# Linear attention, RMS norm and a GELU feed-forward in block products: operand addresses, and GpSimd's work moved between the two layers

## The chip, the core and the metric

The kernel runs on one core of a Trainium2 chip. What counts is the device time of one execution in microseconds, on this one core. Four engines work side by side and meet through semaphores: TensorE (PE; matmuls, with the weight loads that precede them), VectorE (DVE), ScalarE (ACT) and GpSimd (POOL). SyncE (SP) issues most of the DMA transfers. Every engine takes its instructions in program order.

## The reference

```python
# attention: 8 batches, 8 heads, 576 tokens, 64 features a head
kv = np.einsum('bhsd,bhse->bhde', k, v)
out = np.einsum('bhsd,bhde->bhse', q, kv)
rms = np.sqrt(np.mean(out * out, axis=-1, keepdims=True) + 1e-06)
attn = out / rms * g_norm
# feed-forward on the 8*576 = 4608 tokens, 512 features, 2048 hidden
x = attn.transpose(0, 2, 1, 3).reshape(4608, 512)
h = x @ w_in
g = 0.5 * h * (1.0 + erf(h / sqrt(2)))
result = g @ w_out
```

All of it is in 32-bit floats. Nearly all arithmetic is in the two products with `w_in` (512x2048) and `w_out` (2048x512).

## The kernel before

**Precision.** Each float32 factor is split into a high part and the low rest (`hi`, `lo`; a cast on ScalarE, a subtraction on VectorE or GpSimd). A product is then three matmuls: hi x hi, lo x hi, hi x lo.

**Chunks.** The 4608 tokens are nine chunks `c` of 512. Chunks 0 and 1 (`PLAIN` = 2) use plain matmuls of 512 columns for both layers (L655 and L682). From chunk 3 (`FAST` = 3) on, both layers use a Strassen-Winograd scheme: a product of 2x2 blocks in seven block products. Its operands are sums and differences of blocks, and the results are added up again. Chunk 2 is between: its first layer is in block products (`layer1_pair`), its second is plain, and beside it the operands for the later chunks' second layer are made from `w_out`: `sum_out` on GpSimd, `split_out` (a cast on ScalarE, L1199, and a low on VectorE, L1200), and `send`, which writes them to device memory from ScalarE's DMA queue.

**A chunk from 3 on.** Its *first layer* has eight pairs `j`. Each has a `first_part` (block products 0 to 3) and a `second_part` (4 to 6), staggered: first part of `j`, then second part of `j-1`. All their matmuls are at L523, in `product`: 128 weights columns, 256 moving columns. VectorE adds up the results (`add`, L514; the first result is copied out of PSUM at L560) and ScalarE applies the GELU (L579). The *second layer* (class `Fast`) has 28 *ticks* of 12 matmuls each (L1140); a tick is one block product `k` for a quarter `n` of the hidden features, in the order `TICKS`. Ahead of a tick, `ready` makes its operand: `hi` on ScalarE (L1117), `lo` on VectorE (L1118). `combine` (L1107) makes the sums among the hidden blocks.

**The next chunk** is prepared meanwhile. Within the first layer (`within_layer1`, called after each second part): its projections (attention's `q` times `kv`, L230; the split of `q` has its low on GpSimd, L217), their squares (ScalarE, L240, L241; summed on VectorE, L253), the inverse root (`rsqrt`, small VectorE operations at L277 to L295), and the scaling (`scale`: VectorE spreads the factors by a transpose, L307, GpSimd multiplies, L303). Within the second layer (`within_layer2`): the sums of its blocks (`add_blocks`, L344, four operations on GpSimd at tick 0), and seven pieces (`next_piece`: cast on ScalarE, L349, low at L354, on VectorE for an even piece and on GpSimd for an odd one).

**Weights.** Products of weights come back from device memory through a ring of six tiles (`RING`): when a tile is used up, `fetch` loads the next but five into it, on SyncE's queue. Ring tiles have 48 elements more than others. An operand of the first layer lies 48 elements into its tile, one of the second layer 16. Some products stay in memory (`RESIDENT`), in whatever tiles `take` finds free.

The order is written by hand: each engine's instructions follow the program text. Tiles get their addresses in the order in which they are first used.

Of the kernel before, what the change touches and what calls it, by code (L numbers as in the profile page):

```python
# [37 lines left out]
def linear_attn_rms_gelu_ffn(  # L38
# [63 lines left out]
    def late_tile(name):  # L102

        if name not in late:
            late[name] = const.tile([P, 2 * DM], I32, name=name).bitcast(F32)
        return late[name]
# [19 lines left out]
    def load_kv(b, p):  # L126
# [10 lines left out]
        if b == 0:  # L137
            tails = late_tile(f"w_in{NF - 1}")[:TAIL].rearrange("p (a n) -> p a n", a=NP)
            if p == 0:
                nc.sync.dma_start(out=tails, in_=kv_tail[0])  # L140
            tail = tails[:, p]
        else:
            if early:
                tail = late_tile(f"w_in{NF - 5}")[:, (p - 2) * 2 * P:(p - 1) * 2 * P]
            elif b == PLAIN + 1 and p > 1:
                if p == 2:
                    kv_ps["tails"] = const.tile([P, 2 * DM], F32, name="w_in12")
# [37 lines left out]
    class Attn:  # L185
# [7 lines left out]
        def load(self, k):  # L193
# [6 lines left out]
            elif self.c == 1 and k:  # L200
                q = const.tile([P, 2 * DM], I32, name=f"w_in{NF - 1}").bitcast(F32)
# [6 lines left out]
        def split_q(self, p, eng=nc.gpsimd):  # L208
            q = self.q.pop(p)
            if self.c > PLAIN and p % 2:  # L210
                t = const.tile([P, 2 * DM], F32R, name="w_in4")
# [101 lines left out]
        def high_x(self, p):  # L313
            x = const.tile([P, 2, CH], F32R, name=f"x{(NP * self.c + p) % 6}")
            nc.scalar.copy(out=x[:, 0], in_=self.o[p])  # L315
            self.x[p] = x
# [64 lines left out]
    def product_out(at, src, eng=nc.sync):  # L381

        key, n = at[:-1], at[-1]
        if key in RESIDENT and key[0] == "out":
            if key not in resident:
                resident[key] = take(F32R)[1]
# [37 lines left out]
    def high_sums():  # L424

        for (j, second), s in stage.items():
            if j % 2:
                t = reused(second, F32R).rearrange("p (k a n) -> p k a n", k=2, a=2)
            else:
                t = const.tile([P, 2, 2, HALF], F32R, name=f"x{2 + second}")  # L430
# [32 lines left out]
    RESIDENT += [("out", k, GROUPS - 1) for k in ORDER]  # L463
    resident = {}
# [13 lines left out]
    def fetch(n):  # L478

        if n < len(queue):  # L480
# [3 lines left out]
            away = AWAY if key[0] == "in" else AWAY // 3  # L484
# [15 lines left out]
    def take(dtype=F32):  # L500
        name = free.pop(0)
        return name, const.tile([P, 2 * DM], dtype, name=name)

    def keep(key):
        name, t = take(F32R)
        resident[key] = t
# [47 lines left out]
    def first_part(at, j):  # L554
# [5 lines left out]
        nc.vector.tensor_copy(out=u[:, left], in_=a[:, left])  # L560
# [336 lines left out]
    def spread_work(c, i):  # L897
# [31 lines left out]
        for n in {12: (0,), 13: (4, 5), 14: (1, 2), 15: (3, 6)}.get(i, ()):  # L929
            names[c + 1, n] = ("x2", "x3", *(f"w_in{m}" for m in range(5, 10)))[n]  # L930
            t = const.tile([P, 2 * DM], F32R, name=names[c + 1, n])
# [340 lines left out]
    def within_layer1(c, j):  # L1272
# [3 lines left out]
        aft = attn[c + 2] if c + 2 < NCH else None  # L1276
        if nxt:
            if j < NP:
                nxt.project(j, bank("a0"))
                nxt.squares(j)  # L1280
                if j < 2:
                    nxt.split_q(2 + j)
            if j == NP:
                ps = bank("a0")
                nxt.inv = nxt.rsqrt(nxt.fold(ps))
        if c + 2 < B:
            if j == 2:
                kv_ps[c + 2, 0] = bank("a1")
                sum_kv(c + 2, (0, 1), kv_ps[c + 2, 0])
            if j in (2, 3):  # L1290
                load_kv(c + 2, j)
            if j == 5:
                sum_kv(c + 2, (2, 3), kv_ps[c + 2, 0])
                split_kv(c + 2, range(NP))
        if aft:
# [4 lines left out]
        if nxt and j in (5, 6):  # L1300
            nxt.scale(2 * j - 9, nc.gpsimd)
        if c == FAST and j < 2:
            send()
            raw_out(NJ2 - 2 + j)
            free.extend(f"w_out{NF - 4 + 2 * j + n}" for n in range(2))
# [8 lines left out]
    def within_layer2(c, layer, i):  # L1314
# [5 lines left out]
        if c + 1 < NCH:  # L1320
            step = len(layer.ticks) // 8
            if i == 0:
                for k in ("T3", "T1", "T2", "T4"):
                    attn[c + 1].add_blocks(k, nc.gpsimd)
            if i % step == step - 1 and i // step < NPR:
                n = i // step
                next_piece(c, n, nc.gpsimd if n % 2 else nc.vector)

    free += ["x4", "x5", "x0", "x1", "w_in12"]
    for c in range(PLAIN, FAST):  # L1330
        for j in range(NJ2):
            s = c * NF + 2 * j
            pair = layer1_pair(attn[c], j, [lambda e=e: ahead(c, j, e) for e in range(2)])
# [16 lines left out]
            if c == FAST - 1:  # L1350
                if j:
                    free.extend(f"w_out{n}" for n in (2 * j - 2, 2 * j - 1) if n < NF - 4)
                if j == 1:
                    free.append(names.pop("g"))
                send()
                if j > 3:
                    keep(RESIDENT[j - 4])
            ahead_loads(c, j)
    for c in range(FAST, NCH):
# [3 lines left out]
        for j, second in parts_of_layer1():  # L1363
            if not second:
                first_part(at, j)
                if (c, j) == (FAST, 0):
# [4 lines left out]
                    free.extend(f"w_in{n}" for n in (13, 14, 15))  # L1371
# [68 lines left out]
```

## Time and profile before

| | |
|---|---|
| runs, median (lowest to highest) | 842.97 us (842.86 to 845.91), 3 runs |
| the profiled execution's own time | 843.54 us |
| its span, first to last instruction | 841.8 us |
| GpSimd busy in the span | 267.8 us (32%) |
| DMA queue of SyncE (q1) | 235.96 MB, 79.4% of 16 engines |
| TensorE's granted clock | 1.000 |

Up to about 316 us the span holds the splitting of the weights and chunks 0 to 2. Chunk 3 begins then; from there each chunk takes some 90 us, half of it per layer. A profile row names a group of instructions by line, engine, operation and tiles, with its count, busy time and mean duration. A timeline row gives the start, the duration of the group (matmuls overlap, so the distance of starts, not the duration of one, says how fast they follow each other), and in brackets how long the engine had been idle before, and what released it.

### The profile page before, as it was taken

Reading aid. Unit: us, or ns where it says so; the run is one execution under the profiler, and the core shown is the slowest. Engines: PE = TensorE matmul, PEld = TensorE weight load, DVE = VectorE, ACT = ScalarE, POOL = GpSimd, SP = SyncE. Lnnn points to the kernel's source line nnn. Section 1 sums busy time; section 2 is a strip of 40 time slices with the busy share of each in tenths; the row PEclk is TensorE's granted clock in tenths of the full one; section 3 lists DMA queues with packets and bytes.
Section 4 is the critical chain, followed back from the end, with each engine's and each line's share of the span. In section 5 each row is a group of like instructions: output and inputs, shape, how many; then the busy total and the mean of one; then the engine's idle time right before and its main releaser. Section 6 shows DMA issues by size and latency. Waiting matters only on the chain.

```text
span 841.8 us, 16154 instructions
## 1 busy us (share of the span) xinstructions
PE 807.5 (96%) x6248; PEld 751.7 (89%) x6248; DVE 613.7 (73%) x1063; ACT 354.9 (42%) x654; POOL 267.8 (32%) x198
## 2 busy tenths in 40 slices
PE   8999999999998999989998999989998999899998
PEld 7688887888987889889998999989998999899998
DVE  3899737777548865699478946896589758975783
ACT  3788443444532433454143704352335333441351
POOL 1000020102465452274037503552255424541200
PEclk9999999999999999999999999999999999999999
DMA  9971347997796989989988898889897998799984
GB/s 356 408 311 51 113 132 270 361 322 278 274 336 215 321 320 350 398 286 322 341 344 280 293 362 305 307 266 317 274 325 256 308 311 294 242 313 323 325 293 158
DMA packets 90512, 245.39 MB, mean 292 GB/s; under 512 B 9028, under 2 KB 30788, under 8 KB 90436
## 3 DMA queue, kind: packets, MB, share of 16 engines
q1 hardware_dynamic: 85824, 235.96, 79.4%
q10 hardware_dynamic: 4612, 8.39, 2.6%
q8 instruction: 50, 0.82, 0.4%
q14 instruction: 26, 0.21, 0.1%
HBM read 205.52 MB, written 35.13 MB: 286 GB/s over the span
## 4 chain that ended last, share of the span: by engine, by line
PE 74%; DVE 18%; DMA 4%; ACT 2%; issue 1%; POOL 0%; SPq 0%; ACTq 0%; DVEq 0%
PE acc L1140 15%; PE acc L523 13%; PE acc L682 12%; PE h L523 11%; PE h L655 10%; PE a L1140 8%; DVE w_out L1118 4%; PE a L230 3%; DMA w_in<-products_in 2%; DVE acc L514 2%; DVE sq L307 2%; DVE w_out L1107 1%; PE a L169 1%; DVE gl L514 1%; DMA kv_main<-kv_main 1%
## 5 line engine op out<-in xcount | busy, mean ns | idle before, releaser
L1140 PE MATMUL acc<-w_in,w_out 128*128 128x256 f32 x900 | 114.0, 281 | 12.8 <-DVE w_out L1118 12.8
L523 PE MATMUL acc<-w_out,w_in 128*128 128x256 f32 x930 | 119.5, 281 | 3.0 <-DVE gl L514 2.8
L1140 PEld LDWEIGHTS acc<-w_in,w_out 128*128 128x128 f32 x900 | 108.9, 189 | 14.7 <-DVE w_out L1118 14.7
L523 PEld LDWEIGHTS acc<-w_out,w_in 128*128 128x128 f32 x930 | 113.4, 188 | 4.5 <-DVE gl L514 3.5
L682 PE MATMUL acc<-w_out,gh 128*128 128x512 f32 x312 | 97.5, 394 | 0.0
L655 PE MATMUL h<-x,w_in 128*128 128x512 f32 x360 | 87.9, 393 | 0.0
L655 PEld LDWEIGHTS h<-x,w_in 128*128 128x128 f32 x360 | 67.5, 188 | 14.9
L217 POOL TENSOR_TENSOR ql<-q,qh 128x512 fp32r<-128x512 f32 x16 | 21.3, 1334 | 170.5 <-ACT qh L216 170.5
L523 PE MATMUL h<-w_out,w_in 128*128 128x256 f32 x558 | 71.9, 281 | 0.0
L682 PEld LDWEIGHTS acc<-w_out,gh 128*128 128x128 f32 x312 | 58.0, 188 | 12.3
L523 PEld LDWEIGHTS h<-w_out,w_in 128*128 128x128 f32 x558 | 68.2, 188 | 0.1
L682 PE MATMUL acc<-w_out,gl 128*128 128x512 f32 x156 | 61.3, 393 | 1.8 <-DVE gl L674 1.8
L1118 DVE TENSOR_TENSOR w_out<-w_in,w_out 128x512 fp32r<-128x512 f32 x51 | 53.9, 1066 | 2.9 <-ACT w_out L1117 2.9
L668 ACT ACTIVATE gh<-h 128x512 fp32r<-128x512 f32 x39 | 23.2, 596 | 74.5 <-PE h L655 56.0
L354 POOL TENSOR_TENSOR w_out<-z,w_out 128x512 fp32r<-128x512 f32 x5 | 37.8, 7563 | 34.0 <-ACT w_out L349 34.0
L253 DVE TRANSPOSE_TENSOR_REDUCE part<-sq 128x16 f32<-128x512 f32 x33 | 23.4, 709 | 32.5 <-ACT sq L240 32.5
L579 ACT ACTIVATE x<-h 128x512 f32<-128x512 f32 x8 | 4.8, 598 | 100.0 <-DVE h L514 100.0
L674 DVE TENSOR_TENSOR gl<-h,gh 128x512 fp32r<-128x512 f32 x39 | 26.8, 687 | 26.6 <-ACT h L669 22.2
L523 PE MATMUL h<-w_in,w_in 128*128 128x256 f32 x294 | 38.5, 282 | 7.0 <-DVE w_in L514 7.0
L523 PEld LDWEIGHTS h<-w_in,w_in 128*128 128x128 f32 x294 | 36.0, 189 | 8.0 <-DVE w_in L514 8.0
L579 ACT ACTIVATE w_in<-acc 128x512 f32<-128x512 f32 x28 | 16.7, 598 | 54.7 <-DVE acc L514 54.7
L320 POOL TENSOR_TENSOR x<-o,x 128x512 fp32r<-128x512 f32 x5 | 6.5, 1299 | 103.3 <-ACT x L315 103.3
(284 smaller groups left out, 1799.8 us busy)
## 6 DMA issues: line engine op xcount, KB each, us to landing
w_in<-products_in SPq DMA_DIRECT2D x172, 512.0 KB, 5.4
w_in<-products_out SPq DMA_DIRECT2D x126, 512.0 KB, 5.0
kv_main<-kv_main SPq DMA_DIRECT2D x22, 512.0 KB, 6.2
products_in<-w_in SPq DMA_DIRECT2D x40, 256.0 KB, 4.9
w_in<-w_in SPq DMA_DIRECT2D x16, 512.0 KB, 10.2
w_out<-w_out SPq DMA_DIRECT2D x16, 512.0 KB, 10.2
q<-qT SPq DMA_DIRECT2D x15, 512.0 KB, 6.2
products_out<-w_out SPq DMA_DIRECT2D x18, 256.0 KB, 4.3
```

The lines of the kernel that those rows point to most:

```text
L230: nc.tensor.matmul(out=ps[:, a:e], lhsT=w, rhs=x[:, a:e], start=(m == 0), stop=(m == 2))
L253: nc.vector.tensor_reduce(out=self.part[:, p, :], in_=sq.rearrange("p (b d) -> p b d", d=BLK), op=ALU.add, axis=AX.X, apply_transpose=True,)
L354: eng.tensor_tensor(out=x[:, 1], in0=self.block(OPERANDS[n]), in1=x[:, 0].bitcast(F32), op=ALU.subtract,)
L514: eng.tensor_tensor(out=out, in0=x, in1=y, op=op)
L523: nc.tensor.matmul(out=out, lhsT=y, rhs=x[:, z, kb], start=first and kb + i == 0, stop=kb == 1 and i == 2, skip_group_check=True,)
L579: nc.scalar.activation(out=grid(t)[:, :, j % 2], in_=ps.rearrange("p (a n) -> p a n", a=2), func=AF.Gelu)
L655: nc.tensor.matmul(out=h, lhsT=parts["in", i][:, w][:, p * P:(p + 1) * P], rhs=at.x[p][:, x], start=(m + p == 0), stop=(m == 2 and p == NP ...
L668: nc.scalar.activation(out=gh, in_=h, func=AF.Gelu)
L674: nc.vector.tensor_tensor(out=gl, in0=h, in1=gh.bitcast(F32), op=ALU.subtract)
L682: nc.tensor.matmul(out=ps, lhsT=x[:, ts], rhs=parts["out", i][:, w], start=(i == 0 and m == 0), stop=(m == 2 and (i == NF - 1 or (i, t) == ...
L1118: nc.vector.tensor_tensor(out=lo, in0=src, in1=hi.bitcast(F32), op=ALU.subtract)
L1140: nc.tensor.matmul(out=ps[:, a * HALF:(a + 1) * HALF], lhsT=x[:, at], rhs=y, start=(k in (0, 2, 1) and n + p + a + m == 0), stop=(n == GRO ...
```

## The change

- **Addresses.** All tiles of the block products are allocated in a fixed order (`PLACES`), with gaps (`EXTRA`), so that the operands of the first layer's products lie 16 elements, those of the second layer 48 elements beyond a multiple of 64 elements from the blocks that they meet. A float has 4 bytes: the distance is 64 bytes, in one direction, for both layers. Resident products get tiles of their own (`KEPT_IN`, `KEPT_OUT`) in the same grid.
- **GpSimd in the second layer.** The block sums move into the first layer (pairs 5 and 6), and the odd pieces' lows go to VectorE: GpSimd has nothing left in the second layer.
- **Attention at the front.** The four projections come after the second parts 0 and 1, two each; the inverse root after second part 2; the scalings from first part 4 to first part 5. The sums for a later chunk's `kv` move one pair back.
- **The operand of the next tick before the combines**, at odd pairs.
- **The PSUM copy in `first_part`** goes from VectorE to ScalarE.
- **Chunk 2.** `sum_out` and `split_out` follow a table (`SUMS`), `send` moves to the middle of the next pair and issues on SyncE's queue. Sends of raw products move from second parts 0 and 1 of chunk 3 to its start.
- The temporaries of `rsqrt` have one buffer instead of two.

```diff
-    AWAY = 48
+    LINE = 16
+    IN_AWAY, OUT_AWAY = LINE, 3 * LINE
+    KEPT_IN = [f"w_out{i}" for i in (4, 5, 6, 7)]
+    KEPT_OUT = [f"w_out{i}" for i in (8, 9, 10, 11)] + [f"w_in{i}" for i in (13, 14, 15)]
+    RINGS = [f"w_in{i}" for i in RING]
+    PLACES = [f"x{i}" for i in range(6)] + [f"w_in{i}" for i in (4, 5, 6, 7, 8, 9, 12)]
+    PLACES += [f"w_out{i}" for i in (0, 1, 2, 3, 12, 13, 14, 15)]
+    PLACES += RINGS + KEPT_IN + KEPT_OUT
+    EXTRA = {name: 4 * LINE for name in RINGS}
+    EXTRA[RINGS[-1]] += IN_AWAY
+    EXTRA[KEPT_IN[-1]] = OUT_AWAY - IN_AWAY
+    EXTRA[KEPT_OUT[-1]] = 4 * LINE - OUT_AWAY
...
     def block_tile(name, dtype):
-        ring = name in [f"w_in{i}" for i in RING]
-        return const.tile([P, 2 * DM + (AWAY if ring else 0)], dtype, name=name)
+        return const.tile([P, 2 * DM + EXTRA.get(name, 0)], dtype, name=name)
+
+    for name in PLACES:
+        block_tile(name, F32)
...
-                work.tile([P, NP * NB], F32, name=a, bufs=2)[:, :ps.shape[1]]
+                work.tile([P, NP * NB], F32, name=a)[:, :ps.shape[1]]
...
+    SCALES = [(4, False), (3, True), (5, False), (4, True)]
...
-            away = AWAY if key[0] == "in" else AWAY // 3
+            away = IN_AWAY if key[0] == "in" else OUT_AWAY
...
-        name, t = take(F32R)
-        resident[key] = t
+        t = resident[key] = block_tile(KEPT_IN[key[1]], F32R)[:, :2 * DM]
...
-        nc.vector.tensor_copy(out=u[:, left], in_=a[:, left])
+        nc.scalar.copy(out=u[:, left], in_=a[:, left])
...
-                product_out(*x, nc.scalar)
+                product_out(*x)
...
-    def within_layer1(c, j):
+    def within_layer1(c, j, second):
...
-            if j < NP:
-                nxt.project(j, bank("a0"))
-                nxt.squares(j)
-                if j < 2:
-                    nxt.split_q(2 + j)
-            if j == NP:
-                ps = bank("a0")
-                nxt.inv = nxt.rsqrt(nxt.fold(ps))
-        if c + 2 < B:
-            if j == 2:
+            for p in {(0, True): (0, 1), (1, True): (2, 3)}.get(at, ()):
+                nxt.project(p, bank(f"a{p % 2}"))
+            for p in {(0, True): (0, 1), (1, True): (2, 3)}.get(at, ()):
+                nxt.squares(p)
+                if p < 2:
+                    nxt.split_q(2 + p)
+            if at == (2, True):
+                nxt.inv = nxt.rsqrt(nxt.fold(bank("a0")))
+            if at in SCALES:
+                nxt.scale(SCALES.index(at), nc.gpsimd)
+            for k in {(6, False): ("T3", "T1"), (5, True): ("T2", "T4")}.get(at, ()):
+                nxt.add_blocks(k, nc.gpsimd)
+        if second and c + 2 < B:
+            if j == 3:
...
-        if nxt and j in (5, 6):
-            nxt.scale(2 * j - 9, nc.gpsimd)
-        if c == FAST and j < 2:
-            send()
-            raw_out(NJ2 - 2 + j)
...
-            if i == 0:
-                for k in ("T3", "T1", "T2", "T4"):
-                    attn[c + 1].add_blocks(k, nc.gpsimd)
             if i % step == step - 1 and i // step < NPR:
                 n = i // step
-                next_piece(c, n, nc.gpsimd if n % 2 else nc.vector)
+                next_piece(c, n, nc.vector)
...
+    SUMS = {0: (0,), 1: (1,), 2: (2, 3), 3: (4,), 4: (5, 6), 7: (7,)}
...
+            def between(e):
+                if e:
+                    send()
+                ahead(c, j, e)
...
-            if c == FAST - 1:
-                if j:
-                    split_out(j - 1)
-                sum_out(j)
+            for n in SUMS.get(j - 1, ()):
+                split_out(n)
+            for n in SUMS.get(j, ()):
+                sum_out(n)
...
+                    for n in (NJ2 - 2, NJ2 - 1):
+                        raw_out(n)
+                    send()
...
-                if j in (6, 7) and c + 1 < NCH:
-                    attn[c + 1].scale(2 * j - 12, nc.gpsimd)
...
-                if j < NJ2 - 1:
-                    within_layer1(c, j)
+            if j < NJ2 - 1:
+                within_layer1(c, j, second)
...
             if second and j % 2:
                 last = j == NJ2 - 1
-                layer.combine(6, j // 2, nc.vector if last else nc.gpsimd)
                 layer.ready(TICKS.index((0, j // 2)))
-                layer.combine(2, j // 2, nc.vector if last else nc.gpsimd)
+                for k in (6, 2):
+                    layer.combine(k, j // 2, nc.vector if last else nc.gpsimd)
```

The order of instructions at three places, as it stands in the program. First VectorE, from the end of chunk 3's first layer into its second. Before, L1107 is the combine, L1118 a tick's low, L354 a piece's low:

```order
L1107 TENSOR_TENSOR w_out_3897<-w_out_3898,w_out_3897 128x512
L1118 TENSOR_TENSOR x_3929<-w_out_3897,x_3929 128x512
L1107 TENSOR_TENSOR w_out_3897<-w_out_3897 128x512
L1118 TENSOR_TENSOR w_out_3967<-w_in_3716,w_out_3967 128x512
L354 TENSOR_TENSOR w_out_3985<-o,w_out_3985 128x512
L1118 TENSOR_TENSOR w_out_3988<-w_out_3897,w_out_3988 128x512
L1118 TENSOR_TENSOR w_out_4005<-w_in_3378,w_out_4005 128x512
L1118 TENSOR_TENSOR w_out_4021<-w_in_3545,w_out_4021 128x512
L1107 TENSOR_TENSOR w_in_3378<-w_in_3378,x_3377 128x512
```

After (the same operations are at L1121, L1132 and L367):

```order
L1132 TENSOR_TENSOR w_out_3973<-w_out_3921,w_out_3973 128x512
L1121 TENSOR_TENSOR w_out_3921<-w_out_3922,w_out_3921 128x512
L1121 TENSOR_TENSOR w_out_3921<-w_out_3921 128x512
L1132 TENSOR_TENSOR w_in_4005<-w_out_3773,w_in_4005 128x512
L367 TENSOR_TENSOR w_out_4023<-o,w_out_4023 128x512
L1132 TENSOR_TENSOR w_out_4026<-w_out_3921,w_out_4026 128x512
L1132 TENSOR_TENSOR x_4043<-w_in_3429,x_4043 128x512
L1132 TENSOR_TENSOR x_4059<-w_in_3605,x_4059 128x512
L1121 TENSOR_TENSOR w_in_3429<-w_in_3429,x_3428 128x512
```

The low that two combines surrounded now stands ahead of both; the combines follow each other. Tick 6 and the first piece keep their places.

Second GpSimd, chunk 3, from the last scalings to the end of its second layer. Before, L303 scales, L217 is a low of `q`, L1107 a combine, L344 a block sum, L354 a piece's low:

```order
L217 TENSOR_TENSOR w_in_3822<-q,w_in_3822 128x512
L303 TENSOR_TENSOR o<-o,sq 128x512
L1107 TENSOR_TENSOR w_in_3716<-w_out_3717,w_in_3716 128x512
L1107 TENSOR_TENSOR w_in_3716<-w_in_3716 128x512
L303 TENSOR_TENSOR o<-o,sq 128x512 x2
L344 TENSOR_TENSOR z<-o 128x512
L344 TENSOR_TENSOR o<-o 128x2x256
L344 TENSOR_TENSOR w<-z,o 128x512
L344 TENSOR_TENSOR z<-o,w 128x512
L354 TENSOR_TENSOR w_out_4039<-o,w_out_4039 128x512
L354 TENSOR_TENSOR w_out_4154<-z,w_out_4154 128x512
L354 TENSOR_TENSOR w_out_4259<-o,w_out_4259 128x512
```

After (L316 scales, L230 low of `q`, L1121 combine, L357 block sum), from the first scaling to the last combine of the first layer:

```order
L316 TENSOR_TENSOR o<-o,sq 128x512 x2
L1121 TENSOR_TENSOR w_in_3604<-w_in_3605,w_in_3604 128x512
L1121 TENSOR_TENSOR w_in_3604<-w_in_3604 128x512
L316 TENSOR_TENSOR o<-o,sq 128x512 x2
L230 TENSOR_TENSOR ql<-q,qh 128x512
L357 TENSOR_TENSOR z<-o 128x512
L357 TENSOR_TENSOR o<-o 128x2x256
L357 TENSOR_TENSOR w<-z,o 128x512
L357 TENSOR_TENSOR z<-o,w 128x512
L230 TENSOR_TENSOR w_in_3852<-q,w_in_3852 128x512
L1121 TENSOR_TENSOR w_out_3773<-x_3774,w_out_3773 128x512
L1121 TENSOR_TENSOR w_out_3773<-w_out_3773 128x512
```

The scalings now go around the combine pair of `n` = 1, the block sums stand ahead of the combine pair of `n` = 2, and the pieces' lows are gone.

Third the stores of chunk 2. Before, on ScalarE, L240 and L241 read a projection, L216 casts `q`, L393 issues a store of a product, L668 is a GELU:

```order
L240 ACTIVATE sq<-a_2400 128x512
L241 ACTIVATE o<-a_2400,half_g 128x512
L393 DMA products_out_0_2446<-x_2386 128x512
L393 DMA products_out_0_2448<-x_2386 128x512
L393 DMA products_out_0_2450<-w_in_2389 128x512
L393 DMA products_out_0_2452<-w_in_2389 128x512
L240 ACTIVATE sq<-a_2423 128x512
L241 ACTIVATE o<-a_2423,half_g 128x512
L216 CAST w_in_2470<-q 128x512
L668 ACTIVATE gh<-h_2464 128x512
```

After, on SyncE, L501 fetches into the ring, L406 stores a product, L217 loads `q`:

```order
L501 DMA w_in_1518<-products_in_2_1637 128x1024
L501 DMA w_in_2108<-products_in_0_1704 128x1024
L406 DMA products_out_0_2532<-x_2424 128x512
L406 DMA products_out_0_2534<-x_2424 128x512
L406 DMA products_out_0_2536<-w_in_2427 128x512
L406 DMA products_out_0_2538<-w_in_2427 128x512
L501 DMA w_in_2110<-products_in_1_1710 128x1024
L217 DMA q<-qT 128x1024
L501 DMA w_in_2238<-products_in_3_1781 128x1024
L501 DMA w_in_1509<-products_in_0_1769 128x1024
```

The four stores have left ScalarE's order and stand between two fetches of the ring.

More of the change, by code (lines that the diff above doesn't have):

```diff
@@ L104, in late_tile @@
         if name not in late:
-            late[name] = const.tile([P, 2 * DM], I32, name=name).bitcast(F32)
+            late[name] = block_tile(name, I32)[:, :2 * DM].bitcast(F32)
         return late[name]
@@ L146, in load_kv @@
                 if p == 2:
[L147 removed]
+                    kv_ps["tails"] = block_tile("w_in12", F32)
                 tail = kv_ps["tails"][:, (p - 2) * 2 * P:(p - 1) * 2 * P]
@@ L200, in load @@
             elif self.c == 1 and k:
-                q = const.tile([P, 2 * DM], I32, name=f"w_in{NF - 1}").bitcast(F32)
+                q = block_tile(f"w_in{NF - 1}", I32)[:, :2 * DM].bitcast(F32)
             else:
@@ L210, in split_q @@
             if self.c > PLAIN and p % 2:
-                t = const.tile([P, 2 * DM], F32R, name="w_in4")
+                t = block_tile("w_in4", F32R)
                 qh, ql = t[:, :CH], t[:, CH:]
@@ L429, in high_sums @@
             else:
-                t = const.tile([P, 2, 2, HALF], F32R, name=f"x{2 + second}")
+                t = piece(block_tile(f"x{2 + second}", F32R))
             nc.scalar.copy(out=t[:, :, 0], in_=s)
@@ L1332, in linear_attn_rms_gelu_ffn @@
             s = c * NF + 2 * j
-            pair = layer1_pair(attn[c], j, [lambda e=e: ahead(c, j, e) for e in range(2)])
+            def between(e):
+                if e:
+                    send()
+                ahead(c, j, e)
+            pair = layer1_pair(attn[c], j, [lambda e=e: between(e) for e in range(2)])
             for k, t in enumerate(pair):
@@ L1349, in linear_attn_rms_gelu_ffn @@
             ahead(c, j, 2)
[L1350 to L1357, printed above, removed]
+            if j == 1:
+                free.append(names.pop("g"))
+            if j in (1, 2):
+                free.extend(f"w_out{n}" for n in (2 * j - 2, 2 * j - 1))
+            if j > 3:
+                keep(RESIDENT[j - 4])
             ahead_loads(c, j)
```

21 lines of the change are left out of this document (11 added, 10 removed).

## The prediction

> **What bounds the kernel now.** First the page: the totals, then the chain that ended last.
>
> ```profile
> span 841.8 us, 16154 instructions
> PE 807.5 (96%) x6248; PEld 751.7 (89%) x6248; DVE 613.7 (73%) x1063; ACT 354.9 (42%) x654; POOL 267.8 (32%) x198
> PE 74%; DVE 18%; DMA 4%; ACT 2%; issue 1%; POOL 0%; SPq 0%; ACTq 0%; DVEq 0%
> ```
>
> TensorE is busy 96% of the span at full granted clock. So time can go in two ways only: its matmuls follow each other faster, or its idle 34 us shrink. The change touches both. The DVE share of the chain says where to look for the idle time. For the share of each stage I read windows: chunk 3's first layer, chunk 4's first and second layer, chunk 8's second layer.
>
> ```profile
> 310.00:362.00 52.00, 50.17 (x449) 47.96 (x449) 33.12 (x68) 18.88 (x35) 15.15 (x12) 1.00 0.98 363
> 402.00:452.00 50.00, 48.84 (x467) 48.27 (x467) 31.56 (x65) 16.79 (x31) 15.29 (x12) 1.00 0.90 330
> 452.00:492.00 40.00, 37.33 (x316) 36.93 (x315) 36.57 (x50) 19.59 (x36) 21.61 (x10) 1.00 0.87 296
> 798.00:842.00 44.00, 39.88 (x340) 39.68 (x338) 26.11 (x44) 15.62 (x29) 0.00 (x0) 0.99 0.67 228
> ```
>
> After the window's length the columns are PE, weight loads, VectorE, ScalarE, GpSimd, the clock, the DMA share and GB/s. In a second layer (third row) VectorE works 36.57 of 40 us, nearly as long as TensorE. In the last chunk, which prepares no other one, GpSimd is idle and VectorE needs 26.11 for 44 operations, 0.59 each instead of 0.73.
>
> The idle time itself: the line views of the two product matmuls name what ended it, with total and number of times, L1140 (second layer) first, then L523 (first layer).
>
> ```profile
>   DVE w_out L1118: 12.8, 9
>   DVE x L1118: 1.0, 1
>   DVE gl L514: 4.0, 4
>   DVE w_in L514: 7.0, 5
> ```
>
> The first two rows, 13.8 us, are ten waits: two in each of chunks 3 to 7, at the front of the second layer. TensorE's timeline shows chunk 3's pair, VectorE's and GpSimd's timelines what lies beside it.
>
> ```profile
> 371.07 1.46 PE L1140 MATMUL acc<-w_in,x 128*128 128x256 f32 x10 [1.03 <-DVE x L1118]
> 374.44 3.81 PE L1140 MATMUL acc<-w_in,w_out 128*128 128x256 f32 x30 [1.67 <-DVE w_out L1118]
> 369.25 1.77 DVE L1118 TENSOR_TENSOR x<-w_out,x 128x512 fp32r<-128x512 f32 x1
> 371.05 1.66 DVE L1107 TENSOR_TENSOR w_out<-w_out 128x512 f32<-128x512 f32 x1
> 372.63 1.75 DVE L1118 TENSOR_TENSOR w_out<-w_in,w_out 128x512 fp32r<-128x512 f32 x1
> 374.31 0.68 DVE L354 TENSOR_TENSOR w_out<-o,w_out 128x512 fp32r<-128x512 f32 x1
> 370.43 1.73 POOL L344 TENSOR_TENSOR w<-z,o 128x512 f32<-128x512 f32 x1
> 372.23 1.60 POOL L344 TENSOR_TENSOR z<-o,w 128x512 f32<-128x512 f32 x1
> 384.08 7.61 POOL L354 TENSOR_TENSOR w_out<-z,w_out 128x512 fp32r<-128x512 f32 x1 [6.74 <-ACT w_out L349]
> ```
>
> While GpSimd adds blocks (L344), the VectorE operations on 128x512 from SBUF take 1.66 to 1.77 us; with GpSimd waiting, the same shape takes 0.68. Both engines stretch each other: one GpSimd operation beside a busy VectorE lasted 7.61. The ten waits are this collision at the moment when the second layer's first operands are due.
>
> **Term 1: the distance of the operands.** From the addresses of the tiles, moving minus stationary address modulo 256 bytes is mixed before: 0 for 1188 of the 4368 product matmuls, 64 for 1080, 128 for 840, 192 for 1260. After it is 192 for all of them. TensorE's timeline, stretches with one distance, starts compared:
>
> ```profile
> 467.03 1.59 PE L1140 MATMUL acc<-w_in,w_in 128*128 128x256 f32 x12
> 468.46 0.75 PE L1140 MATMUL acc<-w_in,w_out 128*128 128x256 f32 x5
> 488.10 1.57 PE L1140 MATMUL acc<-w_in,w_out 128*128 128x256 f32 x12
> 489.51 1.57 PE L1140 MATMUL a<-w_in,w_out 128*128 128x256 f32 x12
> 585.31 3.01 PE L523 MATMUL h<-w_out,w_in 128*128 128x256 f32 x24
> 588.16 0.52 PE L523 MATMUL acc<-w_out,w_in 128*128 128x256 f32 x3
> 530.54 1.52 PE L523 MATMUL acc<-w_out,w_in 128*128 128x256 f32 x12
> 531.90 0.84 PE L523 MATMUL acc<-w_out,w_out 128*128 128x256 f32 x6
> 322.94 3.72 PE L523 MATMUL acc<-w_out,w_in 128*128 128x256 f32 x30
> 326.50 0.75 PE L523 MATMUL acc<-w_out,x 128*128 128x256 f32 x5
> ```
>
> Distance 0: 1.43 us for 12, 119.2 ns each. 64: 1.41 for 12, 117.5. 128: 2.85 for 24, 118.8. 192: 1.36 for 12, **113.3**. But 192 doesn't always give it: the last pair's 30 (18 of them at 192) take 3.56, 118.7 each. Of the 24 stretches of 18 or more matmuls at 192 with no wait in them, 18 run at 113.9 to 114.3 with their first, slower matmuls, two at 117.9, four between. So 192 is worth about 115.4 in the mixture of before, whose mean comes to 117.6. After: 0.75 x 113.4 + 0.25 x 118 = 114.6, a gain of 3.0 ns x 4368 = 13.1 us. Chunk 3's first layer, with its DMA at 0.98, can't run faster: some 450 of the matmuls, 1.3 us less. **Term: -11.8.** Ends: all slow at 118.0, a loss of 1.7; all fast at 113.3, a gain of 18.8.
>
> The Trainium skill (TensorE: Matmul & The Clock Gate, section "Step-by-step: what each phase is for") says that the moving operand and the weight load have independent read ports. By that rule the addresses would not matter and this term would be 0; the trace speaks against it, with 113.3 beside 119.2 ns at the same shape and clock.
>
> **Term 2: the front of the second layer.** The change moves the block sums and three lows per chunk off the second layer's GpSimd, and puts the operand for tick 5 ahead of the combines. What collided at 369 to 374 us then runs at 0.68: the three VectorE operations there shrink from 5.2 to 2.0, against waits of 1.03 + 1.67. VectorE gets three more lows a chunk, 3 x 0.68 = 2.0 us; at 0.59 each, 53 operations are 31 us of 40, so it stays short of TensorE. What is late next: GpSimd's last combines, now queued behind the block sums. It has 18 operations a chunk in the first layer, at 1.29 to 1.77 some 23 to 32 us of 45; laid out by hand, its chain from the first scale on ends 45 to 49.5 us after the chunk's start, and tick 6 is due at about 52. That leaves some 1.5 us. Of 13.8 I take 13 as gone. **Term: -13.** Ends: 0 (the wait changes its name) and -13.8.
>
> **Term 3: the last second parts.** The 4.0 us of L514 <- gl are four waits ahead of the seventh second part, where a low and the transposes of scaling stand in front of the subtraction. These move to the middle of the layer, and eight PSUM copies a chunk leave VectorE. The copy of before, and the nearest ScalarE rows for its new place (smaller and larger):
>
> ```profile
> 449.30 0.42 DVE L560 COPY gh<-acc 128x256 f32<-128x256 f32 x1
> L180 ACT CAST kv_h<-a 64x256 fp32r<-64x256 f32 x12 | 4.4, 363 | 11.8 <-DVE kv_l L181 10.5 <-PE a L169 1.3
> L723 ACT COPY z<-acc 128x512 f32<-128x512 f32 x6 | 3.6, 600 | 4.3 <-PE acc L682 4.3
> ```
>
> So the copy costs 0.36 to 0.60 on ScalarE instead of 0.42; I take 0.42, nothing. ScalarE has 16.8 of 50 us used; with 8 more it has 20. Three pairs of banks cover the lag; uncovered, 48 x 0.2 = 10 us would show. **Term: -3.5**, ends 0 and -4.
>
> **Term 4: chunk 2.** Of its 7.0 us one wait has a plain cause: ScalarE stood behind stores on its own queue.
>
> ```profile
> 236.00 0.60 ACT L240 ACTIVATE sq<-a 128x512 f32<-128x512 f32 x1 [4.72 <-DMA w_in<-products_in]
> 238.17 2.40 PE L523 MATMUL h<-w_in,w_in 128*128 128x256 f32 x18 [1.60 <-DVE w_in L514]
> ```
>
> The stores go to SyncE's queue, so these 1.6 go. There the ring's fetches stand behind them, and a store waits for its low; 3 us of lateness would be hidden by the two tiles already loaded, more not. The other four waits are sums on GpSimd beside VectorE, moved and not removed. **Term: -1.6**, ends +3 and -7.
>
> **The rest.** No matmul is added. The 512-column matmuls lie as before or at distances not shown: 0. One buffer for the three rsqrt temporaries: the next use is a chunk later: 0.
>
> **Sum.** Against the profiled execution's own 843.5 (span 841.8 and 1.7 around it; the median of the runs is 843.0, half a microsecond lower): 843.5 - 11.8 - 13 - 3.5 - 1.6 = 813.6. I forecast **813.5**.
>
> **The rivals.**
> 1. *The distance brings nothing*: the slow spacing of 118 to 119 ns holds throughout, and what ran fast before had another reason: 843.5 - 18.1 = 825.4. For it: the slow stretch at 322.94. Against: three in four are fast. Chance 0.13. The Trainium skill's rule on the ports, above, would give the same time.
> 2. *The waits come back under another name*: GpSimd ends after tick 6 is due, VectorE's in-order queue stands behind its first low. Only terms 1 and 4 remain: 830. For it: 1.5 us of slack and 1.29 to 1.77 per operation. Against: chunk 8's second layer without GpSimd has no such wait. Chance 0.10.
> 3. *Slower*: the four projections now come in two pairs at the front. Each reads a low that GpSimd makes in 1.3 us behind two combines, and TensorE takes its instructions in order. The fourth low is ready by my layout half a microsecond ahead of its use. Every microsecond of lateness is paid five times; from 6 us a chunk on the gain of 29.9 is gone, at 7 it is 843.5 - 29.9 + 35 = 848.6. Against: in the window 402:452 GpSimd is idle 35 of 50 us. Chance 0.04.
> 4. *The change doesn't do what it says*, terms cancel: within 0.5% of 843. Chance 0.05.
>
> Transfers as the new bound: chunk 4's first layer has 50 x 0.90 = 45 us of them at full share; it would shrink to about 48 us, still above.
>
> **How the numbers follow.** The forecast has 0.68, and its own range is 803 to 822: terms 1 and 4 between their ends, a few of the waits left. From 803 to 829, the range takes in rival 1 and half of rival 2; outside lie the other half (0.05), rivals 3 and 4 (0.09) and 0.04 below 803. Half a per cent is about what a measurement of this kernel can tell from no change. Faster by more: 0.68 + 0.13 + 0.10 = 0.91; same 0.05; slower 0.04.
>
> **What would show it.** Term 1: in TensorE's timeline 12 matmuls of a product start 1.36 us after one another, seldom 1.42. Term 2: no wait of L1140's successor line for a low of VectorE, GpSimd's row of the windows at 0 in the second layers, VectorE's lows at 0.68. Term 3: the wait for gl gone. Term 4: no ScalarE idle time for products stores. Wrong would be: starts 1.42 apart everywhere, GpSimd working past the first layer's end, waits for the projections, or a DMA share of 1.0 in the first layers.

## The result, and the profile after

The changed kernel takes 817.5 us in the median (817.34 to 819.2, four runs), the kernel before 842.91 (841.98 to 845.91): a ratio of 0.9697, 95% interval 0.967 to 0.9724. The forecast was 813.5, its range 803 to 829. The profiled execution's span went from 841.8 to 815.5 us.

The page of the changed kernel: totals and chain.

```profile
span 815.5 us, 16193 instructions
PE 797.0 (98%) x6248; PEld 744.9 (91%) x6248; DVE 566.2 (69%) x1030; ACT 369.6 (45%) x702; POOL 202.9 (25%) x183
PE 92%; DMA 3%; DVE 3%; ACT 1%; issue 0%; DVEq 0%; SPq 0%; ACTq 0%
```

VectorE's share of the chain fell from 18% to 3%. Windows of the changed kernel, columns as before the change: chunk 4's first and second layer, chunk 6's and chunk 8's second layer, then three stretches in chunk 2.

```profile
403.00:447.00 44.00, 44.00 (x440) 43.61 (x440) 29.19 (x58) 18.64 (x37) 22.35 (x17) 1.00 0.95 338
447.40:486.80 39.40, 39.40 (x337) 39.40 (x337) 30.02 (x51) 19.98 (x38) 1.88 (x2) 1.00 0.94 333
615.10:653.00 37.90, 37.90 (x337) 37.90 (x336) 30.12 (x51) 19.48 (x36) 4.28 (x4) 1.00 0.94 321
774.00:811.00 37.00, 37.00 (x329) 37.00 (x329) 24.50 (x41) 15.02 (x28) 0.00 (x0) 1.00 0.74 256
262.00:270.00 8.00, 1.92 (x9) 1.92 (x10) 5.72 (x10) 0.37 (x1) 6.84 (x8) 0.60 0.95 322
268.00:272.00 4.00, 3.92 (x18) 3.92 (x19) 0.79 (x3) 0.43 (x1) 3.84 (x5) 0.50 0.51 186
272.00:278.50 6.50, 6.50 (x27) 5.22 (x26) 5.41 (x10) 3.13 (x7) 1.04 (x2) 0.86 0.43 160
```

From chunk 4 on TensorE has no idle time (first four rows). But two second layers with the same matmuls take 39.4 and 37.9 us. And in chunk 2 TensorE stands still for most of 262 to 270 us and then runs at half clock. The waits of TensorE in the changed kernel, all that are longer than a microsecond in total:

```profile
PE h L537 <- DVE w_in L528: 9.7, 3, 7.5
PE acc L696 <- DVE gl L688: 1.8, 1, 1.8
PE h L781 <- DVE w_in L745: 1.1, 1, 1.1
```

The second and third row were there before. The ten waits of the second layer and the four ahead of the seventh second part are gone. The waits of chunk 2 grew from 7.0 us (five) to 9.7 (three).

Where the time went can be read from when chunk 3's second layer begins, the same matmuls in both kernels. TensorE's timeline, before and after:

```profile
362.58 1.69 PE L1140 MATMUL acc<-w_in,w_in 128*128 128x256 f32 x13
```

```profile
363.16 2.05 PE L1154 MATMUL acc<-w_in,w_in 128*128 128x256 f32 x16
```

Up to here the change has lost 0.6 us; everything is won behind it, 26.9 us of span.

### The profile page after: what moved, and what is told of

Read it like the earlier page. It is cut to its first block, busy times and chain, and to the rows that moved or that the text cites. A ratio compares the mean times of both kernels' runs of the same rounds, so it can differ in the third digit from the quotient of the medians.

```text
span 815.5 us, 16193 instructions
## 1 busy us (share of the span) xinstructions
PE 797.0 (98%) x6248; PEld 744.9 (91%) x6248; DVE 566.2 (69%) x1030; ACT 369.6 (45%) x702; POOL 202.9 (25%) x183
## 4 chain that ended last, share of the span: by engine, by line
PE 92%; DMA 3%; DVE 3%; ACT 1%; issue 0%; DVEq 0%; SPq 0%; ACTq 0%
PE acc L1154 20%; PE acc L537 18%; PE h L537 14%; PE acc L696 14%; PE h L669 10%; PE a L1154 8%; PE a L243 3%; PE a L182 2%; DMA w_out<-kv_main 1%; PE h L661 1%; DMA products_out<-w_out 1%; DMA out<-z 1%; DVE w_out L1214 1%; DMA w_in<-products_in 1%; DVE t L299 0%
## 5 line engine op out<-in xcount | busy, mean ns | idle before, releaser
L230 POOL TENSOR_TENSOR ql<-q,qh 128x512 fp32r<-128x512 f32 x16 | 21.2, 1327 | 255.3 <-ACT qh L229 255.3
L1154 PE MATMUL acc<-w_in,w_out 128*128 128x256 f32 x660 | 82.7, 279 | 0.0
L1154 PEld LDWEIGHTS acc<-w_in,w_out 128*128 128x128 f32 x660 | 79.2, 188 | 0.0
L537 PE MATMUL acc<-w_out,w_in 128*128 128x256 f32 x540 | 74.4, 280 | 0.0
L537 PEld LDWEIGHTS acc<-w_out,w_in 128*128 128x128 f32 x540 | 67.5, 188 | 0.3
L537 PE MATMUL acc<-x,w_in 128*128 128x256 f32 x360 | 48.6, 280 | 0.0
L1154 PE MATMUL acc<-w_in,x 128*128 128x256 f32 x360 | 45.8, 279 | 0.0
L537 PEld LDWEIGHTS acc<-x,w_in 128*128 128x128 f32 x360 | 44.7, 188 | 0.3
L1154 PEld LDWEIGHTS acc<-w_in,x 128*128 128x128 f32 x360 | 43.5, 188 | 0.0
L537 PE MATMUL h<-x,w_in 128*128 128x256 f32 x312 | 41.6, 280 | 0.5 <-PE acc L696 0.5
L528 DVE TENSOR_TENSOR gl<-acc,gh 128x256 f32<-128x256 f32 (+1 forms) x66 | 29.2, 442 | 18.3 <-ACT gh L574 14.6
```

Of the source, the lines that this page charges most:

```text
L230: eng.tensor_tensor(out=ql, in0=q, in1=qh.bitcast(F32), op=ALU.subtract)
L528: eng.tensor_tensor(out=out, in0=x, in1=y, op=op)
L537: nc.tensor.matmul(out=out, lhsT=y, rhs=x[:, z, kb], start=first and kb + i == 0, stop=kb == 1 and i == 2, skip_group_check=True,)
L1154: nc.tensor.matmul(out=ps[:, a * HALF:(a + 1) * HALF], lhsT=x[:, at], rhs=y, start=(k in (0, 2, 1) and n + p + a + m == 0), stop=(n == GRO ...
```

## The experiments

Each is the changed kernel with one edit. A single execution of them is compared by its trace; 2 us between single times mean little. The kernel before, run beside them, took 844.4 us in the median for runs 1 to 4, 847.2 once for 5 to 8, and 844.7 once for 9 to 11.

**1 and 2. The distance.** The whole schedule stays; only the places in the tiles move.

```diff
-    IN_AWAY, OUT_AWAY = LINE, 3 * LINE
+    IN_AWAY, OUT_AWAY = 0, 0
```

> The changed kernel with its whole new schedule, but operands of the block products 0 bytes apart (modulo 256) in place of 64. Theory A (the distance sets how fast product matmuls follow each other): starts of 12 matmuls 1.43 us apart everywhere in chunks 3 to 8, about 119 ns each against a mean of about 115.8 in the changed kernel, and so 817.5 + 3.1 ns x 4368 = about 831 us; no wait of TensorE comes back. Rival (addresses don't matter, the fast stretches had another reason): fast and slow stretches as in the changed kernel, 817.5 us within 2.

> The changed kernel with the operands 64 bytes apart in the other direction (moving minus stationary address 64 modulo 256 in place of 192). Theory A by the rows of before at this distance: 1.41 us for 12 matmuls, 117.5 each, no fast stretch at 113.4, about 825 us. Rival (only the size of the distance matters, not its direction): fast and slow stretches as in the changed kernel, about 817.5.

At distance 0 the kernel took 833.64 us in rounds, a ratio to the kernel before of 0.9869 (0.9844 to 0.9895): more than half of the gain is gone (831 was expected), and no wait of the second layers came back. Its TensorE timeline in chunk 8, and windows of chunk 4's and 6's second layer:

```profile
761.43 1.60 PE L537 MATMUL h<-x,w_in 128*128 128x256 f32 x12
762.87 0.88 PE L537 MATMUL h<-w_out,w_in 128*128 128x256 f32 x6
452.00:492.00 40.00, 40.00 (x336) 1.00 0.95 329
624.00:664.00 40.00, 40.00 (x335) 1.00 0.91 311
```

12 matmuls in 1.44 us, 120.0 ns each, in both layers alike; no short spacing anywhere. In the other direction (`3 * LINE, LINE`) 828.74 us and 117.7 ns on average. The addresses matter, and so does the direction. The rivals fall. But "no fast stretch" did not come true in the other direction: twice, 42 product matmuls in a row ran at the short spacing there, in the first layers of chunks 3 and 5. The end of the first of them, in TensorE's timeline:

```profile
345.74 1.52 PE L537 MATMUL h<-x,w_in 128*128 128x256 f32 x12
347.10 0.84 PE L537 MATMUL h<-x,w_out 128*128 128x256 f32 x6
```

That is 1.36 us for 12.

**3 and 4. What GpSimd still may do in the second layer.** One run gives it the odd pieces' lows again, one the block sums at tick 0.

```diff
-                next_piece(c, n, nc.vector)
+                next_piece(c, n, nc.gpsimd if n % 2 else nc.vector)
```

> The changed kernel with the lows of the odd pieces (three a chunk) on GpSimd in the second layer again. Theory B (the ten waits at the second layer's front came from the block sums on GpSimd, which stood beside the first operands' lows): these lows come later, at ticks 5, 11 and 17; VectorE's lows beside them take 1.1 to 1.8 us again, but no wait of TensorE comes back, 817 to 820 us. Rival (any GpSimd work in the second layer starves TensorE, since VectorE has no time left): waits for a low of VectorE in ticks after 5, 1 us or more a chunk, 823 us or more.

```diff
-            for k in {(6, False): ("T3", "T1"), (5, True): ("T2", "T4")}.get(at, ()):
-                nxt.add_blocks(k, nc.gpsimd)
...
+            if i == 0:
+                for k in ("T3", "T1", "T2", "T4"):
+                    attn[c + 1].add_blocks(k, nc.gpsimd)
```

> The changed kernel with the four block sums at tick 0 of the second layer on GpSimd again. Theory B: the waits at ticks 5 and 6 come back, less the one that the new place of tick 5's low spares: 5 x 1.3 to 5 x 2.9, 824 to 832 us. Rival (the waits went because VectorE is earlier in the first layer's end, by the copies and transposes that left it): no wait, 817 to 820 us.

817.38 and 819.52 us, and in neither any wait of a second layer. For the lows that is what theory B said, though most of VectorE's lows beside them stayed at 0.69 us. For the block sums it is not: they were put back where they were, and the waits stayed away. GpSimd's and VectorE's timelines of that run show why, at the front of chunk 4's second layer:

```profile
448.21 1.74 POOL L357 TENSOR_TENSOR z<-o 128x512 f32<-128x512 f32 x1
452.65 1.30 POOL L357 TENSOR_TENSOR z<-o,w 128x512 f32<-128x512 f32 x1
455.22 0.69 DVE L1132 TENSOR_TENSOR w_out<-x,w_out 128x512 fp32r<-128x512 f32 x1 [1.17 <-ACT w_out L1131]
```

GpSimd's last scaling is done by 440 us there, so it comes to the sums early and has them behind it at 453.95, before the first critical low starts at 455.22. That left two readings: the collision is the cause and attention's early place removes it, or VectorE was simply earlier.

**5. The scalings late as well.** To the edit of run 4 comes:

```diff
-    SCALES = [(4, False), (3, True), (5, False), (4, True)]
+    SCALES = [(6, False), (5, True), (7, False), (6, True)]
...
+            elif not second and c + 1 < NCH:
+                attn[c + 1].scale(2, nc.gpsimd)
```

> As the run with the block sums in the second layer, but the four scalings too stand where they stood before the change (first part 6 to second part 6), so that GpSimd's last multiplication again ends at the boundary of the layers and the block sums lie beside the second layer's first lows. The order of the low and the combines, and the copies on ScalarE, stay as changed. Theory B' (the waits come from GpSimd's work beside the lows of ticks 5 and 6; what took them away is that attention stands at the front): VectorE's operations there take 1.3 to 1.8 us again, TensorE waits 1 to 3 us a chunk at ticks 5 and 6 in five chunks, 823 to 832 us. Rival C (the waits went because eight copies and the order of the low made VectorE earlier): no such waits, 817 to 820.

830.83 us. What TensorE's tick matmuls waited for in this run (total, times), and the boundary of chunk 4 on GpSimd, VectorE and TensorE:

```profile
  DVE w_in L1132: 5.0, 3
  DVE x L1132: 4.7, 2
  DVE w_out L1132: 2.1, 3
455.41 1.30 POOL L357 TENSOR_TENSOR w<-z,o 128x512 f32<-128x512 f32 x1
456.79 1.61 POOL L357 TENSOR_TENSOR z<-o,w 128x512 f32<-128x512 f32 x1
455.76 1.50 DVE L1132 TENSOR_TENSOR w_out<-x,w_out 128x512 fp32r<-128x512 f32 x1 [1.17 <-ACT w_out L1131]
457.18 1.77 DVE L1121 TENSOR_TENSOR x<-w_in,x 128x512 f32<-128x512 f32 x1
457.31 1.42 PE L1154 MATMUL acc<-w_in,w_out 128*128 128x256 f32 x10 [0.70 <-DVE w_out L1132]
460.33 1.42 PE L1154 MATMUL acc<-w_in,x 128*128 128x256 f32 x10 [1.37 <-DVE x L1132]
```

The block sums lie beside the low and the combine again, these take 1.50 and 1.77 us, and the waits are back: 11.8 us in eight. The order of the low and the copies on ScalarE were as changed, so they alone don't remove them. Theory B' holds, for the late scalings: the projections stayed at the front in this run.

**6. A bridge over the borders.** The two spacings of the changed kernel change mostly at borders between layers. One matmul more at each border keeps the distance there too (shown for the way into a second layer; the way back has one of `x` with itself):

```diff
+        bridge("a0", operand(c, ("in", NJ2 // 2 - 1, 3))[:, :P], operand(c, ("out", 0, 0))[:, :HALF])
         for i in range(len(layer.ticks)):
```

> The changed kernel with one matmul more at each of the eleven borders between layers (128 by 256 into a bank that nobody reads then), whose operands lie so that the distance of 64 bytes holds across the border too, where it was 0 or 128 for one weight load. Theory D (the slow and the fast spacing are two states that last until something breaks the distance, and a border breaks it): the spacing no longer changes at the borders; it changes only within first layers, where attention's matmuls stand. Whether that leaves more fast stretches or fewer isn't foretold: between 807 (all fast from chunk 4 on) and 824 us (all slow). Rival (the states come from elsewhere): the changes at the borders stay as they are in the changed kernel, 817.5 plus 11 x 0.11 = 818.7.

820.15 us. Windows of chunk 4's and chunk 6's second layer in this run:

```profile
449.40:488.80 39.40, 39.40 (x337) 1.00 0.97 339
617.50:655.50 38.00, 38.00 (x338) 1.00 0.94 322
```

The same layers are long and short as without the bridge. Theory D falls: the one weight load at another distance is not what switches the spacing. What does stays open.

**7 and 8. The wait in chunk 2.** One run moves its sums apart and lets GpSimd wait for the inverse root, the other only returns the stores to ScalarE's queue.

```diff
-    SUMS = {0: (0,), 1: (1,), 2: (2, 3), 3: (4,), 4: (5, 6), 7: (7,)}
+    SUMS = {0: (0,), 1: (1,), 2: (2, 3), 4: (4, 5), 5: (6,), 7: (7,)}
...
-                nxt.scale(2 * (j - 4) + place // 2)
+                nxt.scale(2 * (j - 4) + place // 2, nc.gpsimd if at == (4, 0) else nc.vector)
```

> The changed kernel with another table for the sums of chunk 2 (none at pair 3, two at 4, one at 5), and the first scaling there on GpSimd, so that GpSimd waits for the inverse root before it begins those sums. Theory E (the wait of 7.5 us at 268 us is the inverse root's small VectorE operations, 0.65 to 1.31 us each beside GpSimd's sums and 0.23 without, ahead of the copy that TensorE waits for; the idle time then costs another 3 us by a lower clock): the small operations take 0.23 again, the wait shrinks to under 2 us, the clock stays at 1.0, 808 to 812 us. Rival (the wait belongs to the stores that now stand in SyncE's queue, whose tiles come back late): the wait stays, 815 to 820.

> The changed kernel with the stores of chunk 2's products issued from ScalarE's queue again, at their new place. Theory E: ScalarE idles behind them as before the change (some 5 us at the first of them), a wait of TensorE near 236 us of about 1.6 us comes back, and the long wait at 268 us stays: 818 to 821 us. Rival (SyncE's queue made it): the long wait goes, 808 to 812.

The first took 811.44 us. The inverse root and the wait in the changed kernel (VectorE, GpSimd, TensorE):

```profile
257.02 1.04 DVE L293 TENSOR_SCALAR y<-m 128x64 int32<-128x64 int32 x1
261.13 1.31 DVE L299 SCALAR_TENSOR_TENSOR t<-y 128x64 f32<-128x64 f32 x1
267.15 0.42 DVE L553 COPY w_in<-h 128x256 f32<-128x256 f32 x1
261.10 2.48 POOL L528 TENSOR_TENSOR x<-w_out 128x512 f32<-128x512 f32 x2
268.08 4.21 PE L537 MATMUL h<-w_in,w_in 128*128 128x256 f32 x18 [7.48 <-DVE w_in L528]
```

and in run 7, where GpSimd's sums begin after it:

```profile
256.29 0.23 DVE L299 SCALAR_TENSOR_TENSOR t<-y 128x64 f32<-128x64 f32 x1
257.85 0.23 DVE L299 SCALAR_TENSOR_TENSOR y<-t,y 128x64 f32<-128x64 f32 x1
260.04 0.42 DVE L553 COPY w_in<-h 128x256 f32<-128x256 f32 x1
261.32 2.54 POOL L528 TENSOR_TENSOR x<-w_out 128x512 f32<-128x512 f32 x2
285.24 4.21 PE L537 MATMUL h<-w_in,w_in 128*128 128x256 f32 x18 [3.27 <-DVE w_in L528]
```

The small operations take 0.23 us again, the copy comes 7.1 us sooner, and the wait of 7.48 is gone. From the start of the first to the end of the last of the nine it is 7.7 us in the changed kernel and 2.3 in run 7, so they are 5.4 of the 7.1 us; the rest is their earlier start and the multiplication that went to GpSimd. Another of 3.27 appeared at 285 us, so the clock did not stay at 1.0 throughout. Theory E holds in its cause. Run 8 took 820.52 us: the long wait stayed, so SyncE's queue had not made it. But the wait near 236 us that theory E let come back did not, with the stores at their new place. In its stead came one of 4.2 us at 305 us, behind a store.

**9 and 10. Other distances.** Steps of 32 bytes on both sides of the changed kernel's 192 modulo 256 (`IN_AWAY, OUT_AWAY = 24, 40` and `8, 56`).

> The changed kernel with operands 96 bytes apart (moving minus stationary address 160 modulo 256). The traces so far show 120.0 ns a matmul at distance 0, 118.8 at 128, 117.7 at 64, and two states, 113.3 and 117.9, at 192. Theory F (192 is special, the neighbours behave like their other neighbour): about 118 to 119 everywhere, no fast stretch, 828 to 832 us. Rival (what counts is the distance from 0, and the step from 128 to 192 is gradual): some fast stretches, 818 to 826.

> The changed kernel with operands 32 bytes apart in the changed kernel's direction (224 modulo 256). Theory F: 118 to 120 everywhere, 828 to 834 us. Rival (a stretch between 192 and 0 in which the fast state is the only one, since it differs from the slow one by where the two streams stand to each other): 113.3 everywhere, about 807 us.

831.19 and 830.76 us, with 118.1 and 118.3 ns on average over the product matmuls, and no short stretch in either. Theory F holds for these two. But 192 is not the only distance with the short spacing: run 2 has it at 64, for 84 of 4368 matmuls. At 0, 128, 160 and 224 no trace here shows it.

**11 and 12. A better chunk 2.** To run 7 come three block sums and one more scaling on GpSimd.

```diff
-                nxt.add_blocks(k)
+                nxt.add_blocks(k, nc.gpsimd if k != "T4" else nc.vector)
```

> The kernel with chunk 2's sums apart (811.4), and besides the third scaling's multiplication and three of chunk 2's four block sums moved from VectorE to GpSimd, which idled from 280.5 to 284.4 there while VectorE had 8 us of work ahead of the copy that TensorE waited 3.3 us for at 285.2. Theory E (VectorE's queue makes that wait): it has 2.8 us less ahead of the copy, the wait shrinks to about 1 us, and with it the half clock after it: 807 to 809 us. Rival (GpSimd's sums now end later, and ScalarE's casts, which need them, stand ahead of the GELU): a new wait of 2 us or more near 290, 811 to 814.

809.69 us. The wait at 282 us shrank to 0.47, as theory E said. A new one of 3.79 came at 293, as the rival said, but for another reason: ScalarE's casts stood behind a store that held their tile, not behind GpSimd's sums. TensorE's timeline (`issue`: the profile names nothing that ended the wait):

```profile
281.88 2.33 PE L537 MATMUL h<-w_in,w_in 128*128 128x256 f32 x18 [0.47 <-DVE w_in L528]
293.47 1.78 PE L537 MATMUL h<-x,w_in 128*128 128x256 f32 x12 [3.79 <-issue]
```

The clock fell all the same, to 0.50 from 294.76 to 298.17 us. Against run 7 it is a tie. Timed in rounds:

> The kernel of the run before (chunk 2's sums apart, three block sums and a scaling there on GpSimd), timed in rounds. If its single 809.7 holds, its ratio to the kernel before is 0.957 to 0.962, clear of the changed kernel's 0.967 to 0.972; if chunk 2's gain was one lucky execution, the intervals overlap.

811.4 us (810.56 to 812.87), a ratio to the kernel before of 0.9606, 95% interval 0.9585 to 0.9627. As expected, that is clear of the changed kernel's 0.967 to 0.9724, and the best of this study.

## Why the prediction was right, and where its sizes were off

**The bound** was read rightly: TensorE's spacing and its idle time were the two sources, and both gave.

**Term 1** (-11.8) was right in mechanism and too large. Run 1 shows that the distance is the cause. The step that failed was "0.75 x 113.4 + 0.25 x 118 = 114.6": three quarters was the share among 24 long stretches, and it was taken for all product matmuls. Counted over the product matmuls of chunks 2 to 8 in groups of six, the changed kernel has 319 short groups, 378 long ones and 18 mixed, a mean of 115.75 ns, against 117.5 before. That is 1.75 x 4368 = 7.6 us, not 13.1. The kernel before already showed the lower share: of its 202 groups at distance 192 without a wait, 94 are short, 78 long and 30 mixed, less than half short, as after the change. With the 115.4 that the prediction itself gave for 192 the term would have been 2.2 x 4368 = 9.6 us. Why a matmul at 192 runs at one spacing or the other stays open. By the rule of independent read ports in the Trainium skill (TensorE: Matmul & The Clock Gate, section "Step-by-step: what each phase is for") this term would have been 0; the trace contradicts it, with 120.0 ns at distance 0 and 113.3 at 192 for the same matmuls at full clock.

**Term 2** (-13) came out: all 13.8 us of idle time went, and a little more, since a stop also costs a restart: the wait of 1.67 us at 374.44 us in the kernel before set the starts back by 1.94. The reason given was only half right. It named the move of the sums and the lows off the second layer; runs 3 and 4 show that each could be undone alone once attention stands at the front (both together were not run), and run 5 that with late scalings the sums bring 11.8 us back. The slack was sized well: GpSimd's last combine ended 46.5 us after chunk 4's start, in the stated 45 to 49.5, and tick 6 began at 53.0. So GpSimd did work past the first layer's end (1.88 and 4.28 us in the windows of second layers above), which the prediction had named as a sign of being wrong though its own layout implied it; it cost no wait.

**Term 3** (-3.5) came out: the four waits of 4.0 us are gone. The move of the transposes was not needed: in run 5 they stand where they stood before, and these waits stay away. Whether the copies on ScalarE removed them was not tested apart.

**Term 4** (-1.6) had the wrong sign. The wait behind ScalarE's stores went, as worked out. The step that failed was "The other four waits are sums on GpSimd beside VectorE, moved and not removed": in their new places two sums ran back to back beside the inverse root, of whose nine small operations all but the first stretched from 0.23 to as much as 1.31 us (in the kernel before, five), ahead of the copy that TensorE needed. The idle time grew by 2.7 us, and the half clock after it cost some 3 more: 18 matmuls took 4.21 us where they take 2.1. The range had +3 for this term, without the clock.

The errors partly cancel: term 1 gave 4 us less than stated, term 4 took some 6 to 7 us more, terms 2 and 3 with the restarts and the small waits for transfers in chunk 3 gave some 5 to 6 more, and about 2 us are not assigned. These are estimates from the distances of starts. The measured gain is 25.4 us for a forecast of 29.4; that it came so near owes something to luck, since the errors had opposite signs.

**The rivals.** Rival 1 (no gain from the distance) is half true: long spacing for half of the groups. Rivals 2, 3 and 4 did not happen: no wait at the boundary, no wait for a projection. Transfers reached a share of 0.95 in chunk 4's first layer and did not bind.

## What to carry to other kernels

Before a collision between two engines is treated by moving work off one of them, look at when that work is free to run: here it was enough to make its inputs early, and the engine got to it earlier by itself. A chain of tiny operations is a bad neighbour for a busy GpSimd, since each one is stretched and their sum stands ahead of whatever is queued behind them. And when matmuls of one shape show two spacings at full clock, compare the operands' addresses before anything else, but count on the spacing that you can force, not on the one that occurs most often.

## What the runs showed of the hardware that was not expected

**One distance has two spacings.** Mean start-to-start times of a 128x256 product matmul by moving minus stationary address modulo 256 bytes: 120.0 ns at 0, 118.8 at 128 (the kernel before), 118.1 at 160, 118.3 at 224. At 192 there are two, 113.3 and 117.8, in the same kernel on the same tiles. At 64 there are two as well, with a mean of 117.7, but the short one is rare: 12 of 707 groups of six in run 2, 19 of 164 in the kernel before. The changed kernel's TensorE timeline in chunk 8, first and second layer:

```profile
742.25 1.58 PE L537 MATMUL acc<-x,w_in 128*128 128x256 f32 x12
743.67 0.87 PE L537 MATMUL acc<-w_out,w_in 128*128 128x256 f32 x6
781.53 1.52 PE L1154 MATMUL acc<-w_in,x 128*128 128x256 f32 x12
782.89 1.30 PE L1154 MATMUL acc<-w_out,x 128*128 128x256 f32 x10
```

1.42 us for 12 in the one, 1.36 in the other. A spacing can last for hundreds of matmuls; it switched at all six borders from a first to a second layer, at three of the five back, after some waits (run 5), and without a wait inside first layers, beside attention's projections (at 497, 582 and 588 us). Which event chooses it isn't settled; the bridge excludes the single weight load at the border. All product matmuls at 113.3 would be worth another (115.75 - 113.3) x 4368 = 10.7 us.

**A short wait can halve the clock.** After the waits of 7.48 (changed kernel) and 3.27 us (run 7) the matmuls ran at 0.50; after one of 3.03 us in the kernel before they did not. Run 12 has a shorter one that did halve it: a wait of 2.21 us that ends at 299.48 us. Windows of run 7 and of the kernel before, behind the wait, and of run 12, two stretches on either side of the moment when the clock fell:

```profile
285.00:289.00 4.00, 3.76 (x17) 0.50 1.01 372
266.00:269.00 3.00, 2.98 (x22) 1.00 0.95 350
296.23:299.64 3.41, 1.20 (x11) 1.00 1.12 372
299.64:303.05 3.41, 3.41 (x17) 0.50 0.87 338
```

The Trainium skill (TensorE: Matmul & The Clock Gate, section "What's actually happening") puts the idle time after which the clock halves at about 3.4 us, in windows that run freely. The waits of 7.48 and 3.03 us fit that by their length, and 3.27 lies a little below. The 2.21 us of run 12 don't fit an idle time of 3.4: TensorE was busy for 1.20 of the 3.41 us before the clock fell. Nor does the length of the wait alone decide here, since 2.21 us halved the clock and 3.03 did not.
